# Retention scores taken by blocks of 64 rows, and in other visits, so that the two kinds of quarter product are even in number in each visit

## The chip, the cores and the metric

The kernel runs on one core of a Trainium2 chip. The metric is device time in microseconds (us) of one execution, the median of several. The engines that matter here: TensorE (PE in the profile, its weight loads PEld), VectorE (DVE), ScalarE (ACT), GpSimd (POOL), and SyncE (SP), which issues the DMAs. They run side by side, each through its own list of instructions in order, and wait for each other by semaphores.

## The reference

Three stages follow each other for 8 batches of 576 tokens, in float32. Only the first is touched by the change; the second, attention, shares its time with it.

```python
# stage 1: retention, 8 heads of 64; rel = i - j, gamma_h near 1
scores = q @ k.T / 8
ret = scores * where(rel >= 0, gamma_h ** rel, 0)
x = concat_heads(ret @ v)                              # (8, 576, 512)
# stage 2: 4 attention experts on x, causal, top 2 of 4 mixed per token by a gate
q, k, v = x @ wq[e], x @ wk[e], x @ wv[e]
ye = softmax(causal(q @ k.T / 8)) @ v @ wo[e]
x = sum over the token's 2 experts of weight * ye
# stage 3
theta = x @ w_theta
u = x + w_tok_r @ (x * cos(theta)) + w_tok_i @ (x * sin(theta))
out = u + relu(u @ w_ch)
```

## The kernel before, in words

**Retention is computed by chunks.** Decay over a distance is a product of a power for the row and a power for the column, so retention of a row is what the earlier blocks have summed up (a 64 x 64 state per head, the sum of k times v) plus the causal part inside the block. A block is 64 rows, a chunk 128 rows, two blocks; the fifth and last chunk of a batch (c = 4) has one block, so a batch has blocks 0 to 8. There are four kinds of product, each 64 x 64 x 64 and so a quarter of the 128 x 128 array:

- *scores* (line 144, `ret_scores`): k of a block times its q, into a bank `w`; DVE then multiplies by the causal mask (line 148) into `sm`.
- *state* (line 160, `ret_state`): adds one block's k times v to the bank `pS`; ACT copies it to `S` (line 163). The next block's state product adds to the same bank and so waits for that copy.
- *values inside the block* (line 173) and *values from the state* (line 180), both in `ret_values`, into one bank `px`; DVE scales it to `xt` (line 190), ACT rounds it to `xh` (192), POOL takes the rest `xl` (193). Behind `xl` in the same function POOL scales the v of a later chunk (`vp`, line 129, in `scale`).

Two heads stand in the two halves of the partitions. Scores and state of the head in half s write half s of the bank: they use the two quarters on the diagonal of the array. Values are written to half 1 - s: the two quarters off the diagonal. So each kind of product comes in pairs, one per half, and a pair of the diagonal kind can lie beside a pair of the other kind, in all four quarters.

**Who sets the order.** On TensorE the order is written out by hand. `ret_step` visits one chunk c of a batch: it takes one diagonal pair and one off-diagonal pair in turn (`zip_longest`) as long as both lists have some; what is left of the longer list follows alone. Below, a *step* is such a turn: a *full* step has both pairs, a *half* step has one alone. In the middle of a visit stands `mid`: the attention outputs that are due (`at_out`, line 387, which multiplies the transposed probabilities `PT` by V). When both `mid` and a following state product exist, the first part takes only 12 off-diagonal pairs; the rest, with the state products, come behind `mid`.

On the other engines a scheduler sets the order when the program is built; it is fixed from then on.

**The loop.** A period of ten slots holds one batch of attention, and in slots 3, 4, 5, 7 and 8 the visits c = 0 to 4 of the next batch's retention (`SLOTS`, "R1" to "R5"). A slot: scores of one attention tile (line 321), which DVE masks and reduces (324) and ACT exponentiates (329); some projections (lines 102 to 104, 259; `U` copies 242 and 245); transposes of the tile before (368), which DVE copies to `PT` for one head and ACT for the other (373, and 375 for the diagonal block); then the visit. Beside all this DVE, ACT and POOL convert a float64 weight table in pieces: on DVE these are lines 456, 459, 457, 461, 462.

**Visits before the change.** Visit c of batch b holds the state products of its second block, the scores of chunk c + 1 (from c = 4 those of the next batch's chunk 0), the values of chunk c, and the state product of chunk c + 1's first block. In pairs: scores 8 for a full chunk, state 4 per block, values 16 (12 for c = 0, 8 for c = 4).

**Memory.** Banks `w` are a ring of 7. The masked scores `sm` are two fixed buffers. Inputs of a chunk (`kt` for q and k, `kv`) are a ring of 4 and are loaded by SP when `ret_values` of the chunk four places earlier is done (lines 118, 121).

Of the kernel before, what the change touches and what calls it, by code (L numbers as in the profile page):

```python
# [10 lines left out]
F32 = mybir.dt.float32  # L11
# [9 lines left out]
B, H, S, D = 8, 8, 576, 64  # L21
E, DM = 4, 512
C = 128
NCH = 5
ROWS = [128, 128, 128, 128, 64]
# [37 lines left out]
def tile_kernel(ctx: ExitStack, tc: tile.TileContext, qk, kv, w1, wo, wot, wd, cst, out):  # L63
    nc = tc.nc
    consts = ctx.enter_context(tc.tile_pool(name="consts", bufs=1))

    def pool(name, **kw):
        return tc.alloc_tile_pool(name=name, bufs=1, **kw)
# [12 lines left out]
    ret = pool("ret", side="right")  # L81
# [5 lines left out]
    tri = att.tile([128, 64], F32, name="tri")  # L87
# [8 lines left out]
    gt = ret.tile([128, 4, S], F32, name="gt")  # L96
    SB = [ret.tile([128, 4, D], F32, name=f"S{i}") for i in range(4)]

    SMT = [ret.tile([128, 2, 4, 64], F32, name=f"sm{i}") for i in range(2)]

    def mm3(ps, ah, al, bh, bl, first, last):
        nc.tensor.matmul(ps, ah, bh, start=first, stop=False)  # L102
        nc.tensor.matmul(ps, ah, bl, start=False, stop=False)  # L103
        nc.tensor.matmul(ps, al, bh, start=False, stop=last)  # L104
# [6 lines left out]
    MARK = {}  # L111
    QKT, KVT, XT, PSS, VP, SM, RAW = {}, {}, {}, {}, {}, {}, []
# [20 lines left out]
    def half(x):  # L133
        return slice(x * 64, x * 64 + 64)

    def ret_scores(b, c):

        n = ROWS[c] // 64
        t = QKT[b, c]
        ps = ps1.tile([128, n, 4, 64], F32, name="w", bufs=WB, padded_shape=[128, 2, 4, 64])  # L140
        for j in range(n):
            for x in range(4):
                for s in range(2):
                    nc.tensor.matmul(ps[half(s), j, x, :], t[half(s), 4 + x, half(j)], t[half(s), x, half(j)],  # L144
                                     start=True, stop=True, skip_group_check=True)
                yield
        sm = SMT[(b * NCH + c) % 2]
        MARK["sm"] = nc.vector.tensor_mul(sm[:, :n], ps, tri[:, None, None, :].to_broadcast([128, n, 4, 64]))
        SM[b, c] = sm

    def ret_state(b, k):

        c, j = divmod(k, 2)
        u, vp = KVT[b, c], VP[b, c]
        if k == 0:
            PSS[b] = ps1.tile([128, 4, D], F32, name="pS", bufs=1, padded_shape=[128, 4, 128])
        pS = PSS[b]
        for x in range(4):
            for s in range(2):
                nc.tensor.matmul(pS[half(s), x, :], u[half(s), j, 0, x * D:x * D + D], vp[half(s), j, x, :],  # L160
                                 start=k == 0 and x == 0, stop=False, skip_group_check=True)
            yield
        MARK["S"] = nc.scalar.activation(SB[(k + 1) % 4], pS, AF.Copy)

    def ret_values(b, c):

        R = ROWS[c]
        t, vp, sm = QKT[b, c], VP[b, c], SM.pop((b, c))
        px = ps1.tile([128, 4, R], F32, name="w", bufs=WB, padded_shape=[128, 4, 128])
        for j in range(R // 64):  # L170
            for x in range(4):
                for s in range(2):
                    nc.tensor.matmul(px[half(1 - s), x, half(j)], vp[half(s), j, x, :], sm[half(s), j, x, :],
                                     start=j == 0 and x == 0, stop=False, skip_group_check=True)
                yield
        for j in range(R // 64):
            k = 2 * c + j
            for x in range(4 if k else 0):
                for s in range(2):
                    nc.tensor.matmul(px[half(1 - s), x, half(j)], SB[k % 4][half(s), x, :], t[half(s), x, half(j)],  # L180
                                     start=False, stop=False, skip_group_check=True)
                yield
        for x in (QKT, KVT, VP):
            x.pop((b, c))
        cs = slice(c * C, c * C + R)
        if c == 0:
            XT[b] = (w1p.tile([128, 4, S], F32R, name="xh", bufs=1),
                     w1p.tile([128, 4, S], F32R, name="xl", bufs=1))
        xt = ret.tile([128, 4, R], F32, name="xt", bufs=2, padded_shape=[128, 4, 128])
        MARK["xt"] = nc.vector.tensor_mul(xt, px, gt[:, :, cs])  # L190
        xh, xl = XT[b]
        MARK["xh"] = nc.scalar.activation(xh[:, :, cs], xt, AF.Copy)  # L192
        MARK["xl"] = nc.gpsimd.tensor_sub(xl[:, :, cs], xt, xh[:, :, cs])  # L193
        nx = (b, c + LDB) if c + LDB < NCH else (b + 1, c + LDB - NCH)
        if nx[0] < B:
            loads(*nx)
        if RAW and (b or c):
            with tc.issue_after(MARK["xl"].ins):
                scale()

    def ret_step(b, c, nx, mid=None):

        diag, off = [], []
        if 0 <= c < NCH - 1:
            diag.append(ret_state(b, 2 * c + 1))
        if nx:
            diag.append(ret_scores(*nx))
        if c >= 0:
            off.append(ret_values(b, c))
        last = nx and nx[1] < NCH - 1  # L210
        off = chain(*off)
        for _, _ in zip_longest(chain(*diag), islice(off, 12) if last and mid else off):
            pass
        if mid:
            mid()
        for _ in zip_longest(ret_state(nx[0], 2 * nx[1]) if last else (), off):
            pass


# [203 lines left out]
    def make_gt(c):  # L423
        R = ROWS[c]
        nc.vector.tensor_mul(gt[:, :, c * C:c * C + R], gt[:, :, :R], gf[:, :, c, None].to_broadcast([128, 4, R]))
# [85 lines left out]
            mm3(acc, wt[:, 0, p, :], wt[:, 1, p, :], th[:, 0, :], th[:, 1, :], kt == 0, kt == 3)  # L511
        split(MH[:, p, :], ML[:, p, :], acc)

    ret_step(0, -1, (0, 0))
    ret_step(0, 0, None)
    for k in range(2):
        with tc.issue_after(MARK["xt"].ins), tc.issue_after(MARK["xh" if k else "S"].ins):
            split_w1(512, slice(2 * k, 2 * k + 2))
# [3 lines left out]
    work(-1, "v0")  # L522
    with tc.issue_after(MARK["split"].ins):
        make_gt(1)
    ret_step(0, -1, (0, 1))
    scale()
    with tc.issue_after(MARK["pool"].ins):
        nc.gpsimd.dma_start(cm, cst[:, o:o + 1088])
    with tc.issue_after(MARK["sm"].ins):
        make_gt(2)  # L530
    ret_step(0, 1, (0, 2))
    for c in range(3, NCH):
        with tc.issue_after(MARK["xt"].ins):
            make_gt(c)
    ret_step(0, 2, (0, 3))
    for k in range(4):
        with tc.issue_after(MARK["xt"].ins), tc.issue_after(MARK["xh"].ins):
            split_w1(0, k)
    w1s.release()
    work(-1, "v1")  # L540
    ret_step(0, 3, (0, 4))
    work(-1, "v2 k00")
    ret_step(0, 4, (1, 0))
    work(-1, "q00 v3 k01 v4 g")


# [85 lines left out]
    for t in range(nu + 1):  # L632
        b, k = divmod(t, 10)
        if b < B - 1:
            more, between, after = *SLOTS[k], ""
        else:
            b = B - 1
            more, between, after = LAST[t - 10 * b]
        if t < nu:
            at_scores(units[t])  # L640
            work(b, more)
            if units[t][2] == NCH - 1:
                at_norm(*units[t][:2])
        if t == nu - 1:
            assert not jobs[1]
            cvt.release()
            atk.release()
            zp = pool("zp")
        if between == "O":
            for o in outs:  # L650
                at_out(*o)
            outs = []
        if t:
            at_trans(units[t - 1])
            ub, up, um = units[t - 1]
            if GROUPS[GRP[um]][-1] == um:
                outs.append((ub, up, GRP[um]))
        if b < B - 1:
            if between[:1] == "R":
                c = int(between[1])  # L660
                x = b + 1
                def mid():
                    for o in outs:
                        at_out(*o)
                    outs.clear()

                ret_step(x, c - 1, (x, c) if c < NCH else (x + 1, 0) if x + 1 < B else None, mid)
        else:
            work(b, between)
            for o in outs:  # L670
                at_out(*o)
            outs = []
        work(b, after)


        i = int(t >= JOBS[0])
        x = t - JOBS[0] if i else t - 2
        while jobs[i] and (x + 1) / due[i] >= njobs[i] - len(jobs[i]) + 1 - 1e-6:
            with ExitStack() as es:
                for e in ("dve", "act"):  # L680
                    es.enter_context(tc.issue_after(MARK[e].ins))
                jobs[i].pop(0)()
        if t == nu - 11:
            assert not jobs[0]
            ret.release()
            w2 = pool("w2")
            WOH, WOL, MH, ML = [w2.tile([128, 2, DM], F32R, name=x) for x in ("WOH", "WOL", "MH", "ML")]
            wol = pool("wol")
            wa = pool("wa")
            fuse_load()  # L690
            load_o(0)
            load_o(1)
        if t == nu - 7:
            w1p.release()
            wa.release()
            w2b = pool("w2b")
            TK = w2b.tile([128, 9, 2, S], F32R, name="TK")
            wk1 = pool("wk1")
            for kt in KORD:
                nc.sync.dma_start(TK[:, kt].bitcast(F32), TD[kt])  # L700
# [253 lines left out]
```

## Time and profile before

| what | value |
| --- | --- |
| median of 3 runs | 892.21 us (891.45 to 894.62) |
| the profiled execution | 891.7 us, its span 889.5 us |
| PE busy | 862.3 us (97% of the span) |
| DVE busy | 619.7 us (70%) |
| ACT busy | 464.2 us (52%) |
| POOL busy | 220.2 us (25%) |
| DMA | 130.28 MB, mean 146 GB/s |
| granted TensorE clock, mean | 0.996 |

The span is the time from the first to the last instruction in the trace; the run's own time is 2.2 us longer. The busy share of PE says that the engine nearly always has something in flight, not that all of the array is used: a pair of quarter products keeps it as busy in this count as two pairs. Retention visits of batches 1 to 7 lie between 55 us and 400 us, one batch in about 52 us; the stage behind them ends the kernel and is not touched.

### The profile page before, as it was taken

What the parts mean: (1) busy time and instruction counts of PE and PEld (TensorE: products, weight loads), DVE (VectorE), ACT (ScalarE), POOL (GpSimd) and SP (SyncE); (2) the same over time, 40 slices, a digit from 0 to 9 for tenths busy, and PEclk for the clock granted to TensorE, in tenths of its full rate; (3) what the DMA queues carried; (4) which work ended last, traced back from release to release, by engine and by line L of the source; (5) the groups of instructions that cost most, each with busy time, mean ns of one, the idle gap of its engine ahead of it and who ended that gap; (6) DMA issues with size and microseconds to landing.
All of it is one profiled execution on the core that took longest, in us unless ns stands there. A gap on an engine that the chain in (4) does not pass through costs nothing.

```text
span 889.5 us, 25515 instructions
## 1 busy us (share of the span) xinstructions
PE 862.3 (97%) x10072; PEld 803.6 (90%) x10072; DVE 619.7 (70%) x1709; ACT 464.2 (52%) x1272; POOL 220.2 (25%) x268
## 2 busy tenths in 40 slices
PE   7899999999999999999999998999999999999998
PEld 6898989888898889888879997999999999999998
DVE  3487778778788886877768686776477764776622
ACT  2375666666666666766667344354244533444320
POOL 2325154443535444352300112010120102101010
PEclk9999999999999999999999999999999999999999
DMA  9758566776767666637783035524426124251311
GB/s 317 234 144 253 156 216 179 193 230 177 247 161 212 191 190 218 173 93 229 215 295 135 23 86 107 113 50 118 120 51 143 38 66 107 37 129 25 87 44 54
DMA packets 147606, 130.28 MB, mean 146 GB/s; under 512 B 84000, under 2 KB 123168, under 8 KB 147488
## 3 DMA queue, kind: packets, MB, share of 16 engines
q1 hardware_dynamic: 147344, 128.39, 51.9%
q8 instruction: 79, 1.29, 0.6%
q0 software_dynamic: 144, 0.28, 0.2%
q14 instruction: 39, 0.32, 0.1%
HBM read 78.03 MB, written 32.00 MB: 124 GB/s over the span
## 4 chain that ended last, share of the span: by engine, by line
PE 83%; DVE 9%; DMA 3%; ACT 2%; issue 2%; SPq 1%; POOL 0%; ACTq 0%; POOLq 0%; DVEq 0%
PE acc L757 23%; PE w L102 9%; PE w L103 9%; PE w L104 9%; PE w L321 5%; PE w L259 5%; PE w L387 5%; PE w L368 3%; PE w L757 3%; PE pS L160 3%; DVE b L461 1%; PE w L144 1%; DVE P L324 1%; DMA KK<-KN 1%; PE acc L102 1%
## 5 line engine op out<-in xcount | busy, mean ns | idle before, releaser
L757 PE MATMUL acc<-TK,zh 128*128 128x288 f32 (+2 forms) x896 | 156.5, 297 | 0.5 <-ACT ob L391 0.5
L757 PEld LDWEIGHTS acc<-TK,zh 128*128 128x128 f32 x896 | 132.5, 189 | 0.8 <-issue 0.6
L329 ACT ACTIVATE P<-P,st 128x128 f32<-128x128 f32 (+4 forms) x160 | 95.6, 598 | 42.8 <-DVE st L324 42.5
L757 PE MATMUL acc<-TK,zl 128*128 128x288 f32 (+1 forms) x448 | 95.9, 296 | 0.0
L773 POOL TENSOR_TENSOR ul<-u,uh 128x576 fp32r<-128x576 f32 x16 | 24.4, 1540 | 288.3 <-ACT uh L772 288.3
L324 DVE CUSTOM_DVE_ANT_0 P<-w,cm 128x128 f32<-128x128 f32 (+4 forms) x160 | 71.9, 476 | 11.6 <-PE w L321 11.3
L321 PE MATMUL w<-KK,U 128*64 128x288 f32 (+4 forms) x384 | 76.2, 327 | 0.0
L102 PE MATMUL w<-xh,WH 128*128 128x288 f32 x256 | 76.0, 297 | 0.0
L104 PE MATMUL w<-xh,WL 128*128 128x288 f32 x256 | 75.4, 295 | 0.0
L103 PE MATMUL w<-xl,WH 128*128 128x288 f32 x256 | 75.3, 294 | 0.0
L107 ACT ACTIVATE zh<-cs 128x512 fp32r<-128x512 f32 x64 | 40.3, 630 | 65.1 <-PE acc L757 48.3
L757 PEld LDWEIGHTS acc<-TK,zl 128*128 128x128 f32 x448 | 72.5, 189 | 0.0
L108 DVE TENSOR_TENSOR zl<-cs,zh 128x512 fp32r<-128x512 f32 x64 | 44.1, 689 | 38.7 <-ACT zh L107 38.1
L605 ACT ACTIVATE cs<-cs,quarter 128x256 f32<-128x256 f32 x72 | 36.4, 506 | 62.9 <-DVE cs L603 62.8
L193 POOL TENSOR_TENSOR xl<-xt,xh 128x512 fp32r<-128x512 f32 (+1 forms) x40 | 48.0, 1199 | 85.1 <-ACT xh L192 78.0
L608 DVE SCALAR_TENSOR_TENSOR cs<-cs,x 128x512 f32<-128x512 f32 x72 | 50.7, 706 | 18.5 <-ACT cs L606 17.6
L387 PE MATMUL w<-PT,V 128*64 128x192 f32 (+3 forms) x576 | 56.3, 325 | 5.8 <-DVE PT L373 4.6
L465 POOL TENSOR_TENSOR r<-r,ex 128x192 f32<-128x192 f32 (+1 forms) x51 | 29.4, 577 | 128.8 <-ACT hl L466 50.1
L321 PEld LDWEIGHTS w<-KK,U 128*128 128x128 f32 (+1 forms) x384 | 54.0, 171 | 6.1 <-issue 2.1
L368 PE MATMUL w<-ident,P 128*128 128x128 f32 (+2 forms) x480 | 58.8, 257 | 0.0
L387 PEld LDWEIGHTS w<-PT,V 128*64 128x64 f32 (+1 forms) x576 | 35.7, 135 | 23.6 <-DVE PT L373 6.3
L104 PE MATMUL w<-uh,CH 128*128 128x288 f32 x192 | 56.6, 295 | 0.0
(160 smaller groups left out, 2394.5 us busy)
## 6 DMA issues: line engine op xcount, KB each, us to landing
KK<-KN SPq DMA_DIRECT2D x128, 144.0 KB
kt<-qk SPq DMA_DIRECT2D x32, 512.0 KB
kv<-kv SPq DMA_DIRECT2D x32, 512.0 KB
raw<-wd SPq DMA_DIRECT2D x43, 192.0 KB
xd<-xb SPq DMA_DIRECT2D x126, 64.0 KB
out<-u SPq DMA_DIRECT2D x28, 288.0 KB
u<-xd SPq DMA_DIRECT2D x28, 288.0 KB
td<-hl SPq DMA_DIRECT2D x27, 192.0 KB
```

Source lines behind the costliest of these rows:

```text
L102: nc.tensor.matmul(ps, ah, bh, start=first, stop=False)
L103: nc.tensor.matmul(ps, ah, bl, start=False, stop=False)
L104: nc.tensor.matmul(ps, al, bh, start=False, stop=last)
L193: MARK["xl"] = nc.gpsimd.tensor_sub(xl[:, :, cs], xt, xh[:, :, cs])
L259: nc.tensor.matmul(ps[:R], x[:, kt, cs], W[:, kt, w0:w0 + NV], start=x is xh and W is WH and kt == 0, stop=x is xl and kt == 3)
L321: nc.tensor.matmul(ps[s][:R], U[:, s, rs], KK[:, s, x, j0:j1], start=x == 0, stop=x == 1)
L324: MARK["dve"] = nc.vector.tensor_tensor_reduce(Ps[s][:R, j0:j1], ps[s][:R], cm[:R, o + j0:o + j1], 1.0, st[:R, 0, s:s + 1] if i else 3.0e3 ...
L329: MARK["act"] = nc.scalar.activation(Ps[s][:R, :n], Ps[s][:R, :n], AF.Exp, bias=st[:R, last, s:s + 1], scale=-1.0, accum_out=SUM[p][:R, m, ...
L368: nc.tensor.transpose(tp[:w, j, :], Ps[s][:R, j * C:j * C + w], ident[:R, :R])
L387: nc.tensor.matmul(po[s * 64:s * 64 + 64, c0:], V[:ROWS[j], j, 2 * p + s, :], v, start=j == 0, stop=j == last, skip_group_check=True)
L608: nc.vector.scalar_tensor_tensor(z, cs, -1.0, x2[:, None, ds].to_broadcast([128, 2, 256]), op0=OP.mult, op1=OP.mult)
L757: nc.tensor.matmul(acc[d][j], A[:, dc], TK[:, kt, W, t0:t1], start=q == 0 and n == 0, stop=q == 8 and n == 2)
```

## The change

Scores are now taken for a list of blocks, not for a chunk, and a table `BLOCKS` says which blocks' scores stand in which visit: visit 0 takes block 4, visit 1 blocks 5 and 6, visit 2 blocks 7 and 8, visit 3 blocks 0, 1 and 2 of the next batch, visit 4 its block 3. The length of the first part of a visit follows from the number of off-diagonal pairs less 4, so that the last 4 of them stand beside the 4 state pairs behind `mid`. The first batch has a function of its own, `ret_first`, without `mid`. The two fixed `sm` buffers become a ring of 4. The core of the diff:

```diff
-    def ret_scores(b, c):
-        n = ROWS[c] // 64
-        t = QKT[b, c]
+    def ret_scores(b, ks):
+        n = len(ks)
         ps = ps1.tile([128, n, 4, 64], F32, name="w", bufs=WB, padded_shape=[128, 2, 4, 64])
-        for j in range(n):
+        for i, k in enumerate(ks):
+            t, j = QKT[b, k // 2], k % 2
             for x in range(4):
                 for s in range(2):
-                    nc.tensor.matmul(ps[half(s), j, x, :], ...
+                    nc.tensor.matmul(ps[half(s), i, x, :], ...
                 yield
-        sm = SMT[(b * NCH + c) % 2]
-        MARK["sm"] = nc.vector.tensor_mul(sm[:, :n], ps, tri...)
-        SM[b, c] = sm
+        sm = ret.tile([128, n, 4, 64], F32, name="sm", bufs=4, padded_shape=[128, 2, 4, 64])
+        MARK["sm"] = nc.vector.tensor_mul(sm, ps, tri...)
+        for i, k in enumerate(ks):
+            SM[b, k] = sm[:, i]
...
-    def ret_step(b, c, nx, mid=None):
-        diag, off = [], []
-        if 0 <= c < NCH - 1:
-            diag.append(ret_state(b, 2 * c + 1))
-        if nx:
-            diag.append(ret_scores(*nx))
-        if c >= 0:
-            off.append(ret_values(b, c))
-        last = nx and nx[1] < NCH - 1
-        off = chain(*off)
-        for _, _ in zip_longest(chain(*diag), islice(off, 12) if last and mid else off):
-            pass
-        if mid:
-            mid()
-        for _ in zip_longest(ret_state(nx[0], 2 * nx[1]) if last else (), off):
-            pass
+    BLOCKS = {0: ((0, (4,)),), 1: ((0, (5, 6)),), 2: ((0, (7, 8)),), 3: ((1, (0, 1)), (1, (2,))), 4: ((1, (3,)),)}
+    def ret_step(b, c, mid=None):
+        diag = [ret_state(b, 2 * c + 1)] if c < NCH - 1 else []
+        diag += [ret_scores(b + x, ks) for x, ks in BLOCKS[c] if b + x < B]
+        last = (b, c + 1) if c < NCH - 2 else (b + 1, 0) if c == NCH - 1 and b + 1 < B else None
+        off = ret_values(b, c)
+        n = (12, 16, 16, 16, 8)[c]
+        for _ in zip_longest(chain(*diag), islice(off, n - 4) if last and (mid or c == NCH - 1) else off):
+            pass
+        if mid:
+            mid()
+        for _ in zip_longest(ret_state(last[0], 2 * last[1]) if last else (), off):
+            pass
+    def ret_first(b, c, nx, scores):
+        diag, off = [], []
+        if 0 <= c < NCH - 1:
+            diag.append(ret_state(b, 2 * c + 1))
+        diag += [ret_scores(nx[0], ks) for ks in scores]
+        if nx and nx[1] < NCH - 1:
+            diag.append(ret_state(nx[0], 2 * nx[1]))
+        if c >= 0:
+            off.append(ret_values(b, c))
+        for _ in zip_longest(chain(*diag), chain(*off)):
+            pass
...
-    ret_step(0, 4, (1, 0))
+    ret_first(0, 4, (1, 0), [(0, 1), (2, 3)])
```

Line numbers of the rows below: those of the kernel before, and in the second piece of each pair those of the changed kernel, where scores are line 142, state 159, values 173 and 180, attention outputs 398.

TensorE in visit 0 of batch 3, from the end of its first part to the attention scores behind it; first before, then now (each row counts the products of one turn):

```order
L144 MATMUL w<-kt 64x64 x2
L180 MATMUL w<-kt,S_136 64x64 x2
L387 MATMUL w<-PT,V 64x128 x2
L387 MATMUL w<-PT,V 64x256 x4
L387 MATMUL w<-PT,V 64x128 x2
L160 MATMUL pS<-vp,kv 64x64 x8
L321 MATMUL w<-KK,U 64x288 x8
```

The four state pairs (line 160, eight products in one row) stood alone behind the attention outputs.

```order
L398 MATMUL w<-PT,V 64x128 x2
L398 MATMUL w<-PT,V 64x256 x4
L398 MATMUL w<-PT,V 64x128 x2
L159 MATMUL pS<-vp,kv 64x64 x2
L180 MATMUL w<-kt,S_136 64x64 x2
L159 MATMUL pS<-vp,kv 64x64 x2
L180 MATMUL w<-kt,S_136 64x64 x2
L159 MATMUL pS<-vp,kv 64x64 x2
L180 MATMUL w<-kt,S_136 64x64 x2
L159 MATMUL pS<-vp,kv 64x64 x2
L180 MATMUL w<-kt,S_136 64x64 x2
L332 MATMUL w<-KK,U 64x288 x8
```

The last four value pairs (line 180) have moved from ahead of the attention outputs to behind them, beside the state pairs (rows 4 to 11), and four score pairs are gone from ahead of them.

DVE in visits 3 and 4 of batch 3; first before, from the mask of visit 3's scores to that of visit 4's:

```order
L148 TENSOR_TENSOR sm_140<-w,tri 128x256
L190 TENSOR_TENSOR xt<-w,gt 128x512
...
L461 SCALAR_TENSOR_TENSOR b_3766<-ex,b_3766 128x192
L462 TENSOR_SCALAR ex<-b_3766 128x192
L373 COPY PT<-w 128x2x128
L245 SCALAR_TENSOR_TENSOR U<-w,U 64x288 x2
L375 COPY PT<-w 128x128
L148 TENSOR_TENSOR sm_139<-w,tri 128x512
L190 TENSOR_TENSOR xt<-w,gt 128x4x64
```

Left out are the two masked attention scores (line 324) and the first three conversion instructions (456, 459, 457), the same in both. Now:

```order
L146 TENSOR_TENSOR sm<-w,tri 128x512
L146 TENSOR_TENSOR sm<-w,tri 128x256
L190 TENSOR_TENSOR xt<-w,gt 128x512
...
L472 SCALAR_TENSOR_TENSOR b_3813<-ex,b_3813 128x192
L384 COPY PT<-w 128x2x128
L386 COPY PT<-w 128x128
L256 SCALAR_TENSOR_TENSOR U<-w,U 64x288 x2
L146 TENSOR_TENSOR sm<-w,tri 128x256
L473 TENSOR_SCALAR ex<-b_3813 128x192
L190 TENSOR_TENSOR xt<-w,gt 128x4x64
```

Visit 3 has two masks in place of one ahead of `xt`. In visit 4 both `PT` copies have moved ahead of the last conversion instruction and of the `U` pair. This second move is in batches 1, 3, 4 and 5; in batches 2 and 6 the two copies already stood together.

## Rows read from the trace of the kernel before

**Rows 1.** The page's chain that ended last, share of the span by engine.

```profile
PE 83%; DVE 9%; DMA 3%; ACT 2%; issue 2%; SPq 1%; POOL 0%; ACTq 0%; POOLq 0%; DVEq 0%
```

**Rows 2.** Timeline of PE, batch 3, visits 0 to 2: start, length, instruction, count, idle.

```profile
159.91 0.27 PE L160 MATMUL pS<-vp,kv 64*64 64x64 f32 x2
...
161.47 1.52 PE L387 MATMUL w<-PT,V 128*64 128x128 f32 x16
162.92 0.68 PE L160 MATMUL pS<-vp,kv 64*64 64x64 f32 x16
...
167.93 0.27 PE L160 MATMUL pS<-vp,kv 64*64 64x64 f32 x2 [0.70 <-ACT S L163]
...
173.27 1.73 PE L387 MATMUL w<-PT,V 128*64 128x192 f32 x18 [0.26 <-DVE PT L373]
```

**Rows 3.** Timeline of PE, batch 3, visits 3 and 4.

```profile
181.94 0.27 PE L160 MATMUL pS<-vp,kv 64*64 64x64 f32 x2
...
187.70 0.27 PE L144 MATMUL w<-kt 64*64 64x64 f32 x2
...
189.29 1.08 PE L387 MATMUL w<-PT,V 128*64 128x256 f32 x8 [0.43 <-DVE PT L373]
190.56 0.44 PE L387 MATMUL w<-PT,V 128*64 128x128 f32 x4 [0.18 <-DVE PT L375]
190.92 0.68 PE L160 MATMUL pS<-vp,kv 64*64 64x64 f32 x16
```

**Rows 4.** Timeline of PE, batch 2, visit 3.

```profile
129.83 0.27 PE L160 MATMUL pS<-vp,kv 64*64 64x64 f32 x2
...
130.83 1.10 PE L180 MATMUL w<-kt,S 64*64 64x64 f32 x32
131.86 0.44 PE L387 MATMUL w<-PT,V 128*64 128x128 f32 x4
```

**Rows 5.** Timeline of ACT, batch 3, visits 0 and 1.

```profile
161.21 0.37 ACT L373 COPY PT<-w 128x256 f32<-128x256 f32 x1
...
165.41 0.78 ACT L329 ACTIVATE P<-P,st 64x576 f32<-64x576 f32 x1 [0.73 <-DVE st L324]
```

**Rows 6.** Timeline of PE, batch 2, visit 4.

```profile
136.97 1.30 PE L387 MATMUL w<-PT,V 128*64 128x256 f32 x12 [0.21 <-DVE PT L373]
```

**Rows 7.** Timeline of DVE, batch 3, visits 0 to 2.

```profile
162.79 0.68 DVE L190 TENSOR_TENSOR xt<-w,gt 128x512 f32<-128x512 f32 x1
164.04 0.45 DVE L324 CUSTOM_DVE_ANT_0 P<-w,cm 64x288 f32<-64x288 f32 x1 [0.57 <-PE w L321]
...
166.28 0.34 DVE L456 TENSOR_SCALAR b<-raw 128x192 int32<-128x192 int32 x1
...
169.99 0.25 DVE L459 TENSOR_SCALAR ex<-raw 128x192 int32<-128x192 int32 x1
...
172.80 0.41 DVE L373 COPY PT<-w 128x256 f32<-128x256 f32 x1
```

**Rows 8.** Timeline of POOL, batch 3, visits 0 and 3.

```profile
165.47 1.04 POOL L129 TENSOR_TENSOR vp<-kv,gam 128x512 f32<-128x512 f32 x1
...
186.78 1.06 POOL L129 TENSOR_TENSOR vp<-kv,gam 128x512 f32<-128x512 f32 x1
```

**Rows 9.** Timeline of DVE, batch 2, visit 0.

```profile
114.12 0.58 DVE L456 TENSOR_SCALAR b<-raw 128x128 int32<-128x128 int32 x1
```

**Rows 10.** Timeline of DVE, batch 3, visits 3 and 4.

```profile
184.08 0.69 DVE L190 TENSOR_TENSOR xt<-w,gt 128x512 f32<-128x512 f32 x1 [0.52 <-PE w L180]
...
186.85 1.10 DVE L459 TENSOR_SCALAR ex<-raw 128x192 int32<-128x192 int32 x1
...
188.82 0.42 DVE L373 COPY PT<-w 128x256 f32<-128x256 f32 x1
```

**Rows 11.** Timeline of PE, first batch, visit 4.

```profile
36.72 0.68 PE L160 MATMUL pS<-vp,kv 64*64 64x64 f32 x16 [1.19 <-POOL vp L129]
```

**Rows 12.** Timeline of SP's queue, batch 3, between visits 2 and 3.

```profile
177.08 0.38 SPq L118 DMA_DIRECT2D kt<-qk  x1
```

More of the change, by code (lines that the diff above doesn't have):

```diff
@@ L97, in tile_kernel @@
     SB = [ret.tile([128, 4, D], F32, name=f"S{i}") for i in range(4)]
-    SMT = [ret.tile([128, 2, 4, 64], F32, name=f"sm{i}") for i in range(2)]
     def mm3(ps, ah, al, bh, bl, first, last):
@@ L134, in half @@
         return slice(x * 64, x * 64 + 64)
-    def ret_scores(b, c):
-        n = ROWS[c] // 64
-        t = QKT[b, c]
+    def ret_scores(b, ks):
+        n = len(ks)
         ps = ps1.tile([128, n, 4, 64], F32, name="w", bufs=WB, padded_shape=[128, 2, 4, 64])
-        for j in range(n):
+        for i, k in enumerate(ks):
+            t, j = QKT[b, k // 2], k % 2
             for x in range(4):
                 for s in range(2):
-                    nc.tensor.matmul(ps[half(s), j, x, :], t[half(s), 4 + x, half(j)], t[half(s), x, half(j)],
+                    nc.tensor.matmul(ps[half(s), i, x, :], t[half(s), 4 + x, half(j)], t[half(s), x, half(j)],
                                      start=True, stop=True, skip_group_check=True)
                 yield
-        sm = SMT[(b * NCH + c) % 2]
-        MARK["sm"] = nc.vector.tensor_mul(sm[:, :n], ps, tri[:, None, None, :].to_broadcast([128, n, 4, 64]))
-        SM[b, c] = sm
+        sm = ret.tile([128, n, 4, 64], F32, name="sm", bufs=4, padded_shape=[128, 2, 4, 64])
+        MARK["sm"] = nc.vector.tensor_mul(sm, ps, tri[:, None, None, :].to_broadcast([128, n, 4, 64]))
+        for i, k in enumerate(ks):
+            SM[b, k] = sm[:, i]
     def ret_state(b, k):
@@ L167, in ret_values @@
         R = ROWS[c]
-        t, vp, sm = QKT[b, c], VP[b, c], SM.pop((b, c))
+        t, vp = QKT[b, c], VP[b, c]
         px = ps1.tile([128, 4, R], F32, name="w", bufs=WB, padded_shape=[128, 4, 128])
         for j in range(R // 64):
+            sm = SM.pop((b, 2 * c + j))
             for x in range(4):
                 for s in range(2):
-                    nc.tensor.matmul(px[half(1 - s), x, half(j)], vp[half(s), j, x, :], sm[half(s), j, x, :],
+                    nc.tensor.matmul(px[half(1 - s), x, half(j)], vp[half(s), j, x, :], sm[half(s), x, :],
                                      start=j == 0 and x == 0, stop=False, skip_group_check=True)
@@ L512, in fuse @@
         split(MH[:, p, :], ML[:, p, :], acc)
-    ret_step(0, -1, (0, 0))
-    ret_step(0, 0, None)
+    ret_first(0, -1, (0, 0), [(0, 1)])
+    ret_first(0, 0, None, [])
     for k in range(2):
@@ L524, in tile_kernel @@
         make_gt(1)
-    ret_step(0, -1, (0, 1))
+    ret_first(0, -1, (0, 1), [(2, 3)])
     scale()
@@ L530, in tile_kernel @@
         make_gt(2)
-    ret_step(0, 1, (0, 2))
+    ret_first(0, 1, (0, 2), [(4, 5)])
     for c in range(3, NCH):
@@ L534, in tile_kernel @@
             make_gt(c)
-    ret_step(0, 2, (0, 3))
+    ret_first(0, 2, (0, 3), [(6, 7)])
     for k in range(4):
@@ L540, in tile_kernel @@
     work(-1, "v1")
-    ret_step(0, 3, (0, 4))
+    ret_first(0, 3, (0, 4), [(8,)])
     work(-1, "v2 k00")
-    ret_step(0, 4, (1, 0))
+    ret_first(0, 4, (1, 0), [(0, 1), (2, 3)])
     work(-1, "q00 v3 k01 v4 g")
@@ L665, in mid @@
                     outs.clear()
-                ret_step(x, c - 1, (x, c) if c < NCH else (x + 1, 0) if x + 1 < B else None, mid)
+                ret_step(x, c - 1, mid)
         else:
```

## The prediction

> **What bounds the kernel now.** I read the chain of waits first: 83% of it is PE, DVE 9% [rows 1]. PE runs through its hand-written list with few gaps, so a turn taken out of that list is worth its own length, unless PE then stands at a wait that some other engine ends at a time of its own. The timelines are read for such waits, visit by visit, with batch 3 as the pattern. What to see there: behind visit 1's first part PE waits 0.70 us for ACT's copy of the state, ahead of visit 2's attention outputs 0.26 us for the transposed probabilities by DVE [rows 2], and in visit 4 twice for DVE, 0.43 and 0.18 us [rows 3]. In visit 0 it waits for nothing [rows 2], but narrowly, as shown below.
>
> **What a turn costs.** In visit 3 of batch 2 the eight full steps take 130.83 - 129.83 = 1.00 us, the eight half steps behind them 131.86 - 130.83 = 1.03 us [rows 4]. A full step (0.125) costs no more than a half step (0.129): pairs in the other two quarters of the array come free. Sixteen steps take 2.03 us there, twelve in visit 0 take 161.47 - 159.91 = 1.56 us [rows 2]; so four steps are worth 0.47 us.
>
> **What is removed.** The pairs are the same in number. In batches 1 to 6 the visits had 12 full and 4 half steps; 16 full; 16 full; 8 and 8; 8 and 4: 76 steps. They now have 12, 16, 16, 16 and 8 full ones: 68. Visits 0 and 4 lose four steps each, visit 3 keeps its 16. In batch 7 only visit 0 loses four. The first batch loses four in each of visits 1 and 2 and pays eight more in visit 4. So 6 x 8 + 4 = 52 steps go; at 0.47 us per four that is 6.1 us, if PE paid for every one. DVE gets one mask more per batch (the same elements in six pieces, not five).
>
> **Visits 0 to 2.** The first part of visit 0 now ends at 161.47 - 0.47 = 161.00 and the attention outputs begin. They are eight products of two instructions: two for an older tile, then six for the fresh one, the second of which (the fourth in all) reads ACT's copy, done at 161.21 + 0.37 = 161.58 [rows 5]. The sixteen instructions take 162.92 - 161.47 = 1.45 us, 0.07 less than their row's length [rows 2]; the six fresh products alone take 1.30 - 0.07 = 1.23 us [rows 6]. So the first two take 0.22, the third about 0.25, and PE comes to the fourth at 161.47. With 0.05 for the signal (189.29 - 188.82 - 0.42, [rows 3, 10]) it waits 0.16 us. ACT's copy hangs on attention work ahead of the visit and does not move. Left of the gain: 0.31 us.
>
> It doesn't last. The last value pairs now stand behind the attention outputs, so the bank for `xt` is ready when the state part ends: 162.92 - 0.31 + 0.68 = 163.29, and with 0.04 more for the signal DVE begins at 163.33, not 162.79 [rows 7], 0.54 us later. Queued behind `xt` on DVE are the masked attention scores, which waited 0.57 us for PE until 164.04 [rows 7]; now they wait for `xt`, until 163.33 + 0.68 = 164.01. ACT's exponentials, which waited 0.73 us for DVE [rows 5], and behind them the state copy that ends PE's 0.70 us [rows 2] hang on that: they come no more than 0.03 us earlier. So visit 1 swallows the rest.
>
> Then POOL. `xl` and `vp` follow `xt` and come 0.54 us later too. The conversion's first DVE instruction ended at 166.28 + 0.34 = 166.62, 0.11 us behind the end of `vp` (165.47 + 1.04 = 166.51) [rows 7, 8]; in batch 2 it took 0.58 us [rows 9]; in visit 4 one that takes 0.25 us elsewhere [rows 7] took 1.10 us and ended at 187.95, 0.11 behind `vp` at 187.84 [rows 8, 10]. It is held until POOL's instruction ends, so it ends 0.54 us later. From there to the copy at 172.80 [rows 7] that ends visit 2's 0.26 us, DVE has a full list. Batches 3 and 4 lose 0.54 us each. In batches 2 and 7, where `xt` stood behind another conversion and moves less, I take the middle between 0 and that, 0.27. In batches 1, 5 and 6 no such instruction stands there or PE is not behind DVE; between a gain of 0.31 and a loss of as much I take 0. Sum: 2 x 0.54 + 2 x 0.27 = +1.6 us.
>
> The Trainium skill says of this (SBUF — State Buffer, "SBUF: two separate sides") that DVE, in a two-port mode or with two SBUF inputs, and GpSimd share a pair of ports under an exclusive lock: whoever starts first has it for the whole instruction. That speaks against this change, since it turns a shift of POOL's products into one as long of DVE's list. If the two shared bandwidth instead, the held instruction would lose only a part of what it overlaps, and the sum above would be near zero or a small gain. The two rows that end 0.11 us behind `vp` speak for the lock.
>
> **Visits 3 and 4.** Visit 3 has 16 steps as before, shorter by 0.03 us (8 x 0.004). DVE now has two masks ahead of `xt`; the second becomes ready only with the last pairs and holds `xt` by its length, about half of `xt`'s 0.69 us, with the signal 0.4: 184.08 [rows 10] becomes 184.5. `xl` and `vp` follow and the held conversion with them: +0.4. In batches 1, 3, 4 and 5 the `PT` copy now stands one conversion (about 0.25 us) earlier in DVE's list: it begins at 188.82 [rows 10] + 0.4 - 0.25 = 188.97, and the attention outputs 0.47 us behind it as before, at 189.44 in place of 189.29 [rows 3]. PE is there four steps earlier and only waits longer. But the second copy now follows the first at once, so the second wait goes: the outputs take 1.23 us unbroken and the state part begins at 190.67, not 190.92 [rows 3]: 0.25 us gained, 1.0 in four batches. In batch 2 the copies already stood together and PE waited 0.21 us [rows 6]: 0.4 lost. In batch 6 there is no conversion at that place; of 0.47 us I take 0.3 as gained. Sum: -1.0 + 0.4 - 0.3 = -0.9 us. Bounds: with nothing held longer 0.65 gained in each of the four batches and 0.3 in batch 6, -2.9; with the hold and no relief from the order 0.4 lost in all five, +2.0.
>
> **First batch.** In visit 4 PE waited 1.19 us for `vp` [rows 11]; the eight half steps (1.03) fit in. In visits 1 and 2 the state pairs now stand among the values, so `xt` comes behind them, and by way of `xl` that `vp` too: between -0.3 and +0.6, taken as +0.3.
>
> **Sum.** +1.6 - 0.9 + 0.3 = +1.0 us on the profiled run's 891.7 (889.5 of span and 2.2 around it): 892.7. The median of the runs shown is 0.5 us above that run; I forecast 893.0, between the two.
>
> **The rivals.**
> 1. *Every step pays* (all waits move along with PE): 6.1 us less, 892.2 - 6.1 = 886.1. For it: PE is the chain. Against: the named waits end on DVE's and ACT's time.
> 2. *The steps pay in part*: the conversions escape the hold, since a shift of some tenths can also change which engine starts first. Then visits 0 to 2 gain 0.03 to 0.31 us in seven batches (about 1.0 in all) and visits 3 and 4 gain 2.9: 892.2 - 3.9 = 888.3. For it: at 169.99 [rows 7] such an instruction passes unhindered. Against: in visits 0 and 4 they already ended with `vp`.
> 3. *A load comes too late* (the slower side). Scores of block 2 now stand in visit 3, a visit earlier than before. Their `kt` is issued at 177.08 [rows 12] and used some twelve steps into the visit, 181.94 + 1.56 = 183.50 [rows 3], 6.4 us later. This decides from a landing above 6.4 us; each us more costs one in each of six batches, so 1 us gives 892.2 + 6.0 = 898.2. For it: no wait in the trace of before shows how early this load lands. Against: its place in SP's list is the old one.
>
> **How the numbers follow.** Forecast, with its own range from 890.5 to 895.5: 0.55. Rival 1: 0.08. Rival 2: 0.24. Rival 3, or a hold as long in every visit (7 x 0.54 + 2.0 = 5.8, 898.0): 0.13. The range, 888.0 to 897.0, holds the forecast and most of rival 2 and leaves out rivals 1 and 3. What a measurement of this kernel can tell from no change is about 0.5%, 4.5 us: faster means below 887.7, slower above 896.7. Faster: rival 1 and some of rival 2, 0.15; slower: 0.13; within: 0.72.
>
> **What would show it.** Right: `xt` of visit 0 about 0.5 us later against the visit's start; visit 1's wait near 1.0 us; visit 2's wait for DVE near 1 us in batches 3 and 4; in visit 4 one wait of about 1.1 us and no second; conversions that end 0.1 us behind `vp`. Wrong: visit 2's attention outputs coming as early as before or earlier, counted from visit 0's start; visit 4's wait below 0.7 us; a wait of PE for a DMA in visit 3.

## The result

The kernel after takes 898.1 us (median of 13 runs, 894.5 to 900.8), the kernel before 892.7 in the runs beside them (median of 13, 891.1 to 895.0): ratio 1.0057, 95% interval 1.0044 to 1.0069. It is slower by some 5.4 us. 893.0 was forecast with a range to 897.0, so the result lies outside, on the side of rival 3. The profiled run of the kernel after took 898.1 us, 895.9 of them span, at a mean granted clock of 0.990 (before: 891.7, 889.5 and 0.996).

To compare the traces I set the start of each group of attention transposes on PE against the same group of the kernel before. In batches 1 to 7 the retention visits of the kernel after lose or gain like this (us):

| batch | 1 | 2 | 3 | 4 | 5 | 6 | 7 |
|---|---|---|---|---|---|---|---|
| visit 0 | 0.02 | -0.05 | -0.04 | -0.04 | -0.05 | -0.05 | -0.04 |
| visit 1 | 0.31 | 0.27 | 0.24 | 0.27 | 1.38 | 0.26 | 0.28 |
| visit 2 | 0.00 | 0.63 | 0.45 | 0.42 | 1.84 | -0.01 | 0.35 |
| visits 3, 4 | -0.22 | 0.47 | -0.23 | -0.17 | -0.22 | -0.23 | -0.01 |

The first batch ahead of them loses 0.44. Visits 0 to 2 sum to +6.4 with batch 5 (3.2 of it) and -0.6 come back in visits 3 and 4.

### The profile page after: what moved, and what is told of

Same layout as the page of the kernel before. It is cut to its first block, busy times and chain, and to the rows that moved or that the text cites. A ratio compares the mean times of both kernels' runs of the same rounds, so it can differ in the third digit from the quotient of the medians.

```text
span 895.9 us, 25521 instructions
## 1 busy us (share of the span) xinstructions
PE 863.4 (96%) x10072; PEld 803.2 (90%) x10072; DVE 625.6 (70%) x1715; ACT 467.8 (52%) x1272; POOL 220.6 (25%) x268
## 4 chain that ended last, share of the span: by engine, by line
PE 78%; DVE 10%; DMA 4%; issue 2%; ACT 2%; SPq 2%; POOL 1%; POOLq 0%; DVEq 0%; ACTq 0%
PE acc L768 23%; PE w L100 9%; PE w L101 9%; PE w L102 9%; PE w L270 5%; PE w L398 5%; PE w L332 5%; PE w L768 3%; PE w L379 3%; PE pS L159 2%; DVE P L335 2%; DMA kv<-kv 2%; PE w L142 1%; DVE b L467 1%; DVE b L472 1%
## 5 line engine op out<-in xcount | busy, mean ns | idle before, releaser
L398 PE MATMUL w<-PT,V 128*64 128x192 f32 (+3 forms) x576 | 58.9, 326 | 9.9 <-DVE PT L384 8.9
L398 PEld LDWEIGHTS w<-PT,V 128*64 128x64 f32 (+1 forms) x576 | 37.7, 136 | 28.5 <-DVE PT L384 10.9
```

Source lines behind the costliest of these rows:

```text
L398: nc.tensor.matmul(po[s * 64:s * 64 + 64, c0:], V[:ROWS[j], j, 2 * p + s, :], v, start=j == 0, stop=j == last, skip_group_check=True)
```

## The profile after

The page's chain, against [rows 1]: PE's share is down, DMA's, issue's and SP's are as large or larger, and POOL appears.

```profile
PE 78%; DVE 10%; DMA 4%; issue 2%; ACT 2%; SPq 2%; POOL 1%; POOLq 0%; DVEq 0%; ACTq 0%
```

PE of the kernel after in batch 3, visits 0 to 2, against [rows 2] (PEld is the weight load; start us, length, instruction, count, idle before and its releaser; at visit 0 this kernel is 1.82 us behind the one before):

```profile
162.86 1.94 PE L398 MATMUL w<-PT,V 128*64 128x128 f32 x16
...
163.50 1.05 PEld L398 LDWEIGHTS w<-PT,V 128*64 128x64 f32 x10 [0.23 <-ACT PT L384]
...
170.00 0.27 PE L159 MATMUL pS<-vp,kv 64*64 64x64 f32 x2 [0.95 <-ACT S L162]
...
175.78 1.73 PE L398 MATMUL w<-PT,V 128*64 128x192 f32 x18 [0.40 <-DVE PT L384]
```

The first part of visit 0 is shorter as forecast: it begins at 161.77 and the attention outputs at 162.86, 1.09 us later in place of 1.56. But the sixteen outputs take 1.94 us in place of 1.52. The products of the two heads run side by side, as a narrow stretch of the timeline shows, of before and of after:

```profile
161.73 0.39 PE L387 MATMUL w<-PT,V 128*64 128x256 f32 x2
```

```profile
163.13 0.59 PE L398 MATMUL w<-PT,V 128*64 128x256 f32 x2
```

Before, the third and the fourth of the eight products start together, 0.27 us behind the first (two instructions in 0.39 us, one of each head). After, only the head whose `PT` DVE copies goes on at 163.13 (two instructions of its own, one behind the other, in 0.59 us) and keeps its pace to its end. The other head, which reads ACT's copy, stands from 163.13 to 163.50, 0.37 us, and needs 0.05 more to get going. The 0.23 that the profile names is only the idle time of the weight loads. The outputs end where they ended before, and 0.04 to 0.05 is left of the 0.47.

DVE and POOL there, against [rows 7, 8]:

```profile
165.52 0.69 DVE L190 TENSOR_TENSOR xt<-w,gt 128x512 f32<-128x512 f32 x1 [1.05 <-PE w L180]
166.12 0.44 DVE L335 CUSTOM_DVE_ANT_0 P<-w,cm 64x288 f32<-64x288 f32 x1
...
168.35 1.00 DVE L467 TENSOR_SCALAR b<-raw 128x192 int32<-128x192 int32 x1
```

```profile
168.19 1.06 POOL L127 TENSOR_TENSOR vp<-kv,gam 128x512 f32<-128x512 f32 x1
```

`xt` begins 165.52 - 162.79 - 1.82 = 0.91 us later, not 0.54. The masked scores now queue behind it and begin 0.26 later (166.12 against 164.04 + 1.82), so do the exponentials and the state copy, and visit 1 loses 0.24. `vp` is 0.90 late too, and the first conversion instruction, which took 0.34, takes 1.00 and ends 0.10 us behind `vp` (169.35 and 169.25). That is visit 2's loss. PE's wait there is 0.40 us, not the 1 us that the prediction named as a sign.

PE and DVE in visit 4 of batch 3, against [rows 3, 10]:

```profile
191.96 1.30 PE L398 MATMUL w<-PT,V 128*64 128x256 f32 x12 [1.05 <-DVE PT L384]
```

```profile
191.49 0.41 DVE L384 COPY PT<-w 128x256 f32<-128x256 f32 x1
191.82 0.28 DVE L386 COPY PT<-w 128x128 f32<-128x128 f32 x1
```

One wait of 1.05 us in place of 0.43 and 0.18, then the outputs without a break: this kernel is 2.51 us behind here, and 189.44 + 2.51 = 191.95 was forecast.

Batch 5 is another matter. DVE, PE, and busy times by stretch (the granted clock is the third number from the right, 1.00 for 2.4 GHz):

```profile
271.22 0.26 DVE L467 TENSOR_SCALAR b<-raw 128x192 int32<-128x192 int32 x1 [0.89 <-DMA raw<-wd]
```

```profile
277.26 0.27 PE L159 MATMUL pS<-vp,kv 64*64 64x64 f32 x2 [1.65 <-ACT S L162]
```

```profile
272.00:278.00 6.00, 4.33 (x145) 3.75 (x144) 5.21 (x18) 3.87 (x11) 3.96 (x5) 1.00 0.56 152
278.00:284.00 6.00, 6.00 (x98) 5.60 (x102) 4.81 (x13) 3.59 (x13) 3.90 (x5) 0.57 0.62 179
284.00:290.00 6.00, 6.00 (x108) 5.28 (x101) 3.03 (x8) 2.31 (x8) 1.27 (x2) 0.86 0.81 233
```

In this batch a conversion stands ahead of `xt` on DVE, and it waits 0.89 us for its raw numbers. PE then waits 1.65 us in visit 1 (0.84 in the kernel before), and behind that wait its clock falls from 2.4 to 1.2 GHz: 0.57 granted on the mean from 278 to 284. Together that is 3.2 us. SP's queue tells why the load is late; it stands behind four copies of `KK`, of after and of before:

```profile
264.94 3.38 SPq L248 DMA_DIRECT2D KK<-KN  x4
268.36 0.59 SPq L460 DMA_DIRECT2D raw<-wd  x1
```

```profile
262.18 2.55 SPq L237 DMA_DIRECT2D KK<-KN  x4
264.77 0.60 SPq L449 DMA_DIRECT2D raw<-wd  x1
```

Visit 0 begins at 268.09 after and at 265.33 before: the load is issued 0.27 us behind that start, not 0.56 ahead of it. Why the four issues took 0.83 us longer no run shows; in other runs below they took 2.54 to 4.12 us.

## The experiments

Medians are set against the kernel before in the same series (892.4 in the first, 893.0 in the second and third).

**1. The late `xt` alone, and undone.** One line each:

```diff
# late_xt, from before
-  islice(off, 12) if last and mid else off
+  islice(off, 12 if c else 8) if last and mid else off
# early_xt, from after
-  n = (12, 16, 16, 16, 8)[c]
+  n = (16, 16, 16, 16, 8)[c]
```

late_xt: 

> The kernel before, with one thing of the change alone: in visit 0 the last four value pairs stand behind the attention outputs, as in the kernel after; scores and all other visits are as before, and visit 0 has as many steps as before. Theory A (the loss in visits 0 to 2 comes from xt, which begins about 0.9 us later against the visit: it holds the masked attention scores and with them visit 1, and by xl and vp a conversion on DVE and with it visit 2): +0.25 us in visit 1 and +0.4 to +0.6 in visit 2 of batches 2, 3, 4 and 7, +0.3 in batches 1 and 6, so about +3.3 over the median of the kernel before of 892.7: 896.0, and up to 899 if batch 5 meets the slow clock too. Rival C (the loss comes from the scores that stand in other visits): no change, 892.7 within 1.

Measured 896.2 us against 892.4, ratio 1.0037 (1.0024 to 1.0049). Its profile has visit 1 at +0.23 to +0.29 in all batches but 5 (+0.07), visit 2 at +0.64, +0.44, +0.44 and +0.38 in batches 2, 3, 4 and 7, and nothing anywhere else up to batch 7's end: the same losses in the same places as the kernel after, with no score moved. DVE and PE of batch 3:

```profile
164.89 0.69 DVE L190 TENSOR_TENSOR xt<-w,gt 128x512 f32<-128x512 f32 x1 [0.82 <-PE w L180]
...
167.72 1.00 DVE L456 TENSOR_SCALAR b<-raw 128x192 int32<-128x192 int32 x1
```

```profile
169.37 0.27 PE L160 MATMUL pS<-vp,kv 64*64 64x64 f32 x2 [0.94 <-ACT S L163]
```

The wait of 0.94 and the instruction of 1.00 us are those of the kernel after.

early_xt: 

> The kernel after, with all twelve value pairs of visit 0 ahead of the attention outputs again (four of its steps are half steps, 16 in all); the blocks of scores stay where the change put them. Theory A: visits 0 to 2 lose nothing against the kernel before (xt no later than there, perhaps 0.27 us earlier by the shorter mask ahead of it), batch 5 has no wait for a load and no slow clock; what is left is +0.4 in the first batch and -0.6 in visits 3 and 4: 892.5, with a spread as narrow as that of the kernel before. Rival C (the scores' new places): still 896 or more. Rival B (SP's loads come late against PE whatever xt does, and the clock falls for it): batch 5 still loses 3 us, 895.5.

Measured 894.0, ratio 1.0018 (1.0005 to 1.0030): 1.6 us over the kernel before where the kernel after is 5.4 over it, so 3.8 are back, but not all that was expected. In batch 3:

```profile
165.74 0.68 DVE L190 TENSOR_TENSOR xt<-w,gt 128x512 f32<-128x512 f32 x1
...
169.51 0.24 DVE L467 TENSOR_SCALAR b<-raw 128x192 int32<-128x192 int32 x1
```

```profile
171.15 0.27 PE L159 MATMUL pS<-vp,kv 64*64 64x64 f32 x2 [0.69 <-ACT S L162]
...
176.49 1.72 PE L398 MATMUL w<-PT,V 128*64 128x192 f32 x18 [0.24 <-DVE PT L384]
```

The conversion takes 0.24, the waits are 0.69 and 0.24 as in [rows 2]. Left are two losses: 1.35 us in batch 5, where the conversion waits 1.31 us for its load although `xt` is early (rival B was right about the load, not about the clock, which stays at 2.4 GHz there), and 3.12 us in the first batch, taken up in 4. Theory A stands, rival C falls.

**2. Is DVE held by POOL?**

```diff
- MARK["pool"] = nc.gpsimd.tensor_mul(vp[:, :n], ...)
+ for j in range(n):
+     MARK["pool"] = nc.gpsimd.tensor_mul(vp[:, j], ...)
```

vp_halves: 

> The kernel after, with POOL's product vp in two instructions of half the size. If DVE's conversion is held until POOL's instruction ends, it now gets in between the halves: in visit 0 of batch 3 the first conversion instruction takes 0.6 us or less in place of 1.00, visit 2 comes 0.2 to 0.4 us earlier in batches 2, 3, 4 and 7, about -1.2 in all: 896.9. If both share a bandwidth instead, splitting changes nothing there: 898.1, the conversion instruction stays at 1.0 us.

```profile
171.04 0.58 DVE L468 TENSOR_SCALAR b<-raw 128x192 int32<-128x192 int32 x1
171.54 0.66 DVE L471 TENSOR_SCALAR ex<-raw 128x192 int32<-128x192 int32 x1
```

```profile
170.87 1.22 POOL L128 TENSOR_TENSOR vp<-kv,gam 128x256 f32<-128x256 f32 x2
```

The same instruction in batch 3 takes 0.58 and ends 0.14 us behind the middle of the two halves (171.62 and 171.48); the one behind it is held by the second half in its turn and ends 0.11 us behind it (172.20 and 172.09). Visit 2's loss is gone in batches 3, 4 and 7, half gone in batch 2 (0.33), and new in batch 1 (0.34). So the hold lasts as long as POOL's instruction, as the exclusive lock of the Trainium skill has it (SBUF — State Buffer, "SBUF: two separate sides"): held until POOL's end, not slowed over it. The median did not follow: 897.9, ratio 1.0060 (1.0048 to 1.0072), where 896.9 was expected; this profile lost 3.07 us in the first batch and about 2 behind batch 7's retention, and what the timed runs lost no trace shows.

**3. The late load.**

```diff
  def job(i):
+     load(i)
+     load(i + 1)
-     convert(pl, ..., wd[:, off + o:off + o + n], n)   # issued its load
+     convert(pl, ..., RAWS.pop(i), n)
```

raw_ahead: 

> The kernel after, with each load of the raw numbers issued one conversion earlier in SP's queue. Theory B (about 3 us of the loss are batch 5's: the conversion that stands ahead of xt waits 0.9 us for its load, PE's wait in visit 1 grows to 1.65 us and TensorE's clock drops to 1.2 GHz for some 7 us): the wait for the load is gone, the clock stays at 2.4 GHz in batch 5, about -3 us: 895, mean clock 0.994 or more, and the spread of the runs is narrower. Rival D (the load is by the way, PE's wait and the clock's fall come from the late xt alone): no change, 898.

Measured 894.6, ratio 1.0036 (1.0019 to 1.0053), 2.2 us over the kernel before where the kernel after is 5.4 over it, so 3.2 are back, as expected; the spread didn't narrow (891.8 to 900.2). The profiled run was the longest of the twelve, but its batch 5 gained 0.49 us against the kernel before where the kernel after lost 3.2. PE's wait in visit 1 there, and the clock:

```profile
281.65 0.27 PE L159 MATMUL pS<-vp,kv 64*64 64x64 f32 x2 [0.89 <-ACT S L162]
```

```profile
277.00:283.00 6.00, 5.11 (x160) 4.71 (x151) 4.83 (x16) 3.94 (x10) 3.35 (x4) 1.00 0.89 249
```

Theory B stands for batch 5 as far as this one profile shows it: no late load, no long wait, no slow clock. The wait that went ahead of the fall was the longest: in the profiles of late_xt and vp_halves PE waits 1.46 and 1.49 us at this place and the clock stays at 2.4 GHz.

```profile
276.67 0.27 PE L160 MATMUL pS<-vp,kv 64*64 64x64 f32 x2 [1.46 <-ACT S L163]
278.70 0.27 PE L160 MATMUL pS<-vp,kv 64*64 64x64 f32 x2 [1.49 <-POOL vp L128]
```

**4. The first batch.** It cost 0.44, 3.12, 3.07 and 5.90 us in the four profiles so far that have the change's first batch (after, early_xt, vp_halves, raw_ahead), and nothing in late_xt. PE in early_xt, visit 4 and the projection behind it:

```profile
36.01 0.62 PE L159 MATMUL pS<-vp,kv 64*64 64x64 f32 x13 [0.77 <-POOL vp L127]
38.68 0.45 PE L159 MATMUL pS<-vp,kv 64*64 64x64 f32 x3 [2.05 <-issue]
39.06 0.61 PE L100 MATMUL w<-xh,WH 128*128 128x288 f32 x1
39.47 0.44 PE L101 MATMUL w<-xl,WH 128*128 128x288 f32 x1
```

In the middle of one group of products, before its last three, PE stands for 2.05 us and no releaser is named ("issue"). Behind it the products take 0.44 us where 0.29 is usual: the clock is at 1.2 GHz (granted 0.50 from 40 to 42 us). In the kernel after the stop is at the same product (37.52, 0.30 us). My first theory laid it to the state pairs that the change put among the other steps:

```diff
-     if nx and nx[1] < NCH - 1:
-         diag.append(ret_state(nx[0], 2 * nx[1]))
      ...
+     for _ in ret_state(nx[0], 2 * nx[1]): pass    # behind the steps
```

first_old: 

> The kernel after, with the first batch's state pairs behind the other steps again, as in the kernel before (the blocks of scores stay where the change put them). Theory E (the change makes the first batch's retention a denser stream of instructions, and PE then stands without a wait that the trace shows, 2 to 3 us in visit 4 or visit 2, and its clock drops behind it; in four profiles of kernels with the new first batch that cost 0.4, 3.1, 3.1 and 5.9 us against the kernel before, in the one with the old first batch 0.0): the first batch costs 0.5 or less, about 2 us off the median of 898.1: 896. Rival (the first batch is worth the +0.4 that the profile of the kernel after shows and no more): 897.7.

early_first (with early_xt's line): 

> The kernel after, with both parts taken back: all twelve value pairs of visit 0 ahead of the attention outputs, and the first batch's state pairs behind its other steps; left of the change are the blocks of scores in visits 3 and 4. By the sum of the parts: nothing lost in visits 0 to 2, 0.5 or less in the first batch, -0.6 in visits 3 and 4, and a wait for a load in batch 5 that may come or not (up to 1.3): 891.8 to 893, against 892.4 of the kernel before. If instead the parts don't add up (the first batch's loss is the new scores' own): 894.

Both missed: 899.6, ratio 1.0059 (1.0042 to 1.0077), and 896.5, ratio 1.0024 (1.0009 to 1.0039). first_old's profile has the stop at the same product again, 2.09 us, and 3.87 lost in the first batch; theory E fell. early_first's profiled run took 893.6 and has no such stop; what its longer runs lost no trace shows. What both keep is the block of 32 more products in visit 4. The stops seem to go by count: in the kernel before two of them, 2.50 and 1.06 us, stand 11 + 116 = 127 recorded products apart (21.50 and 27.01). So I moved the whole list by 24:

```diff
- WARM = 50
+ WARM = 26
```

warm_26: 

> The kernel after, with 26 in place of 50 of the products that only keep TensorE busy at the start, so that every later product stands 24 places earlier in PE's list of instructions. Theory F (PE's stops of 2 to 3 us for which the trace names no releaser come at fixed counts, 128 products or a multiple of it after one another, so they are its own instructions being loaded): each such stop comes 24 products later in the work: the one ahead of the last three state pairs of the first batch's visit 4 moves into the projection behind it, 21 products further, and shrinks below 1 us there, since that work takes more time for a product; the one in visit 2 moves by 24 products as well. If the stops belong to the work itself (a load of kt or kv that lands late), they stay ahead of the same products.

```profile
24.93 0.27 PE L173 MATMUL w<-sm,vp 64*64 64x64 f32 x2 [3.46 <-issue]
...
37.63 0.68 PE L159 MATMUL pS<-vp,kv 64*64 64x64 f32 x16 [0.34 <-POOL vp L127]
```

The stop that stood at 21.14 ahead of eleven products now comes behind those eleven and 13 more, 24 in all, inside another group; the one before the last three of visit 4 is gone, those 16 run through, and the projection behind has none. Theory F stands: the stops follow the count of PE's instructions, not the work or a load. In the profiles of all fourteen kernels the first of them stands ahead of the same place in PE's list, after 349 recorded products (348 in vp_halves). The page of the kernel after has the queue that brings the instructions:

```profile
q8 instruction: 79, 1.29, 0.6%
```

That is 79 packets of 16 KiB for PE's 10072 products and as many weight loads, one for some 255 of them. By the packets' own records in the fourteen traces, each of the 29 "issue" stops over 0.25 us in the first 60 us ends 1.26 to 1.61 us after one of these packets has landed. So these stops are waits for a packet of instructions that came late; why it came late no run shows. The rule that fits is in the Trainium skill (Runtime: NRT & Kernel Launch, "Instruction fetch mechanics"): an engine's instructions are refilled in blocks of 256. It calls the cost of a block's edge mostly hidden; here it is 0.3 to 3.5 us. An estimate from its figure is at most 128 products with their weight loads in a block, and 127 were counted. The median, 896.5 (1.0034, 1.0017 to 1.0051), includes a slower start: PE waits 1.09 us for `kt`, and the 32 products behind it take 1.97 us in place of 1.15.

Then the first batch as in the kernel before, its products in the same order (first_old's edit is in it too), with blocks 2 to 6 of the second batch in that batch's own visits 0 and 1:

```diff
- ret_first(0, 4, (1, 0), [(0, 1), (2, 3)])
+ ret_first(0, 4, (1, 0), [(0, 1)])
+ BLOCKS1 = {**BLOCKS, 0: ((0, (2, 3)),), 1: ((0, (4, 5)), (0, (6,)))}
```

after_fs: 

> The kernel after, with the first batch wholly as in the kernel before, its product list the same word for word: visit 4 makes block 0 and 1 of the next batch alone, and the second batch makes blocks 2 to 6 in its visits 0 and 1 (no step more). Theory G (the first batch loses 2 to 4 us because the 32 more products in its visit 4 put a stop of PE, which comes at fixed counts of products, at the end of that visit's fast part, and the clock drops behind it): the first batch costs 0.0 as in the kernel before, the rest stays as in the kernel after (3.3 to 3.9 in visits 0 to 2, -0.6 in visits 3 and 4, batch 5's wait for a load): 2 to 2.5 us under the kernel after, 3 to 3.5 over the kernel before (896). If the first batch's loss is not typical of the timed runs: as the kernel after, 5.5 over the kernel before.

Measured 895.9 against 893.0, ratio 1.0035 (1.0022 to 1.0048), as expected. Visit 4 waits for `vp` as in [rows 11] and has no stop; the first batch costs 0.18:

```profile
36.90 0.68 PE L159 MATMUL pS<-vp,kv 64*64 64x64 f32 x16 [1.19 <-POOL vp L127]
```

Of the seven profiles with the 32 products in visit 4 and the list not shifted, five have that stop, 0.3 to 3.2 us; of six without them none has. vp_halves, which has the 32 products and not that stop, has one of 2.43 us, 127 products behind its first, and the low clock behind it; it lost 3.07 us.

**5. What is left of the change.** Early `xt` and the old first batch together, then the loads ahead as well, and these loads in the kernel before.

early_fs: 

> As the one with the first batch wholly as before, and with all twelve value pairs of visit 0 ahead of the attention outputs. By the sum of the parts: first batch 0.0, visits 0 to 2 0.0, visits 3 and 4 -0.6, batch 5's wait for a load 0 to 1.3: 0.6 under to 0.7 over the kernel before. If the old first batch doesn't help in the timed runs: 1.6 to 3.5 over it.

Measured 893.0 against 893.0, ratio 1.0003 (0.9994 to 1.0013): the parts add up to no change, in its profile visits 3 and 4 gain 0.23 us in most batches, and 1.26 us in batch 5 and 0.78 in batch 3 are lost, the latter with an "issue" stop of 0.56 us at 169.28.

early_raw_first (the change's visit 4 in the first batch): 

> As the kernel with both parts taken back, and with each load of the raw numbers one conversion earlier in SP's queue. By theory B the wait for a load in batch 5 is gone and about 0.5 us more is gained there: 891.0, some 1.4 us under the kernel before. If that load costs nothing once xt is early: 891.8 to 892.5.

early_raw_fs: 

> As the one with the first batch as before and the early xt, and with each load of the raw numbers one conversion earlier: batch 5's wait goes as well, 0.6 to 1.5 us under the kernel before, and a narrower spread than with the first batch of the kernel after.

raw_before: 

> The kernel before, with each load of the raw numbers one conversion earlier and nothing of the change: what that edit is worth by itself. In the profile of the kernel before no conversion waits for its load, so 0.0, within 0.5 of the kernel before; if its timed runs meet that wait too, 0.5 to 1.5 us under it, and then the gain of the best kernel so far is this edit's and not the change's.

Measured 891.7 (0.9984, 0.9969 to 1.0000), 891.1 (0.9982, 0.9970 to 0.9993) and 891.5 (0.9993, 0.9983 to 1.0003). early_raw_fs beats both kernels, the kernel before by some 1.6 us; raw_before can't be told from the kernel before, nor well from early_raw_fs. How much of the 1.6 is the moved scores' stays open.

## Why the prediction was wrong

- *What a turn costs* and the shorter first part: right (1.09 us for the eight steps).
- **The step that failed first** is "PE comes to the fourth at 161.47" in visits 0 to 2, and with it "Left of the gain: 0.31 us". I set the products of the two heads one behind the other. They run side by side: the fourth starts with the third, 0.27 us behind the first (161.73 in the trace of before), so PE was to come to it at 161.27 and to wait 0.36 us, not 0.16. Measured are 0.37 and 0.05 for the restart; 0.04 was left. So `xt` came 0.91 us late, not 0.54 (0.27 of the difference by this, the rest by the state part and the signal behind it), and "they come no more than 0.03 us earlier" turned into masks 0.26 late: 0.24 to 0.31 lost in visit 1 of every batch but 5, where I had nothing.
- The hold of the conversion by `vp`: right as a mechanism (2 and late_xt show it), too small as a size: visits 1 and 2 of batches 3 and 4 lose 0.69, not 0.54, batches 2 and 7 lose 0.90 and 0.63, not 0.27, and batches 1 and 6 some 0.3, not 0. The term was +1.6; late_xt measures it at 3.9 alone. Rival 3's second half, a hold as long in every visit (898.0), was nearest, in part by luck: its +2.0 for visits 3 and 4 was -0.6.
- Visits 3 and 4: -0.9 forecast, -0.6 measured, each batch within 0.1 us of what was worked out for it.
- First batch: +0.3 forecast for a late `xt`. The profile of the kernel after lost 0.44 there, and its timed runs some 2.5 (after_fs), by something that I didn't look for: a stop for PE's own instructions moved to the end of a fast visit, and, in the profiles that lost more, the clock behind it. The "issue" waits stood in the trace of before.
- Batch 5: the sum held no load that comes late and no fall of the clock. 3.2 us in the profile, though not in every run: late_xt and after_fs have nearly nothing there. Rival 3 had a late load, but of `kt` in visit 3: PE waits for none there.

In medians, each against the kernel before in its own series, 3.9 for the late `xt` and 5.4 - 2.9 = 2.5 for the first batch, with the -0.6 of the profile for visits 3 and 4, give 5.8 against the 5.4 measured; each median is known to about 1 us. That leaves nothing for batch 5 in the typical run, while raw_ahead took 3.2 off; what its edit took off beyond batch 5 no run shows.

## What to carry to other kernels

Steps that an engine saves ahead of a wait are worth nothing if that wait is nearer than their length, and what was pushed behind it to save them pays in full: find what the last moved product feeds, and whose queue that stands at the head of. Where two instructions start together in the timeline, the second one's operand is needed at that start, not a product's length later. A moved group of instructions also shifts where a long list of instructions is refilled; "issue" waits at equal counts in the trace of before show where that already hurts. Where a wait grows past what it was anywhere in the trace, ask what the clock does behind it.

## What the runs showed of the hardware

- PE's stops about 127 recorded products or a multiple of it apart: 0.3 to 3.5 us in the first 41 us, each ended 1.26 to 1.61 us after a 16 KiB packet of the instruction queue had landed. Behind 50 us the fourteen profiles have three of 0.3 us or more: 0.30 (raw_ahead, 127.26), 0.56 (early_fs, 169.28) and 0.84 (early_raw_first, 278.47), each 1.38 to 1.53 us after such a packet.
- Of two heads' products side by side, those of one head stood 0.37 us for their operand while the other's ran on; the sixteen instructions took 0.42 us longer, and the profile shows 0.23 of it as idle.
- A DVE instruction of 0.34 us took 1.00 beside POOL's of 1.06 and ended 0.10 us behind it; with POOL's product in two halves it took 0.58.
- After a stop of 1.65 us in the middle of steady work the clock was at 1.2 GHz; waits of 1.46 and 1.49 us at the same place in other profiles left it at 2.4 GHz.
